# Strided q and k rows of batch 0: two a partition on 128 partitions and a short third transfer, in place of three a partition on 96

## The chip, the cores and the metric

The kernel runs on one core of a Trainium2 chip. The time is the device time of one execution in microseconds (us). Engines are called as the profile calls them: PE (TensorE matmul) and PEld (its weight loads), DVE (VectorE), ACT (ScalarE), POOL (GpSimd) and SP (SyncE). Transfers are issued by POOL or SP and carried by 16 DMA engines that all queues share.

## The reference

Eight batches of eight heads, 576 positions, 64 values a head, go through masked attention; the result, laid out as 4608 tokens of 512 values, goes through a two-layer network with a squared ReLU. Heads 0 to 3 look at the last 32 positions, heads 4 to 7 at earlier positions with the same remainder by 32 ("strided").

```python
scores = scale * np.matmul(q, k.transpose(0, 1, 3, 2))
rel = pos[:, None] - pos[None, :]
mask_local = (rel >= 0) & (rel < 32)
mask_strided = (rel >= 0) & (pos[None, :] % 32 == pos[:, None] % 32)
masks = np.stack([mask_local if h < H // 2 else mask_strided for h in range(H)], axis=0)
scores = np.where(masks[None, :, :, :], scores, -1000000000.0)
attn = softmax(scores)                       # over the last axis
x = np.matmul(attn, v).transpose(0, 2, 1, 3).reshape(B * S, H * D)
h = x @ w_in                                 # 512 -> 2048
out = np.maximum(h, 0.0) ** 2 @ w_out        # 2048 -> 512
```

## The kernel before

Work is cut into units (batch, pair of heads); units 0 and 1 of batch 0 are local, 2 and 3 strided. The network runs in nine chunks of 512 tokens: `mm1` (line 678, 64 matmuls a chunk) makes relu squared of `x @ w_in`, `mm2` (line 700) multiplies by `w_out`. Order is written by hand: each engine executes its instructions in program order. The string `BATCH0` lists the steps of the first batch, and `PLAN` lists which attention steps and which loads stand before which group of network matmuls.

Before `BATCH0` stands a setup. SP issues the q and k of unit 0 (`load_qk_hw`, line 275). POOL issues the strided q rows of batch 0 (`load_str_rows`, line 313), builds the identity matrix (`make_identity`), issues the strided k rows (line 313 again), and then cuts the two masks with three selects (lines 851 and 853 for `mask_loc`, 861 for `mask_str`). After these it issues q and k of unit 1 (line 295), v of batch 0 (lines 408 and 580) and the four quarters of `w_in` (line 429). DVE meanwhile fills constants and then turns the masks into additive biases in a corner of `w_out_b` (lines 863, 865, 866). Ten matmuls on zeros (`warm`, line 735) run on PE.

`BATCH0` then runs, on PE in this order: transposes of unit 0's q and k (line 457), after a cast by ACT for q and by DVE for k (line 302); scores of unit 0 (`S0`: bias matmul line 489, score matmuls line 500); the transposes of the strided rows, two groups for q (`W0q0`, `W0q1`) and two for k (`W0k0`, `W0k1`), by `step_TS` at line 336, with copies at line 341; scores of units 2, 3 and 1, sums and outputs; and `P0 P2 P13`, the first network matmuls. `w4`, `w2`, `w3` are more matmuls on zeros between them.

The strided rows: q (or k) of heads 4 to 7 of batch 0 is read as 288 rows of eight positions each, 512 values of fp32, cast to bf16 by the transfer, and lies in `w_out_b` at rows of blocks 4 to 6 (q) or 8 to 10 (k), where the later `w_out` has its place. Before, row 96*s + p is on partition p, block s. A transpose takes 128 columns of one block and all its partitions and puts them into 96 columns of a PSUM tile; six of them fill the 576 columns of a group.

Of the kernel before, what the change touches and what calls it, by code (L numbers as in the profile page):

```python
# [162 lines left out]
def kernel(  # L163
# [9 lines left out]
    nc = tc.nc  # L173
    B, H, S, D = q.shape
# [5 lines left out]
    QL = 96  # L180
    NL = S // QL
    NJ = 8
    RH = STRIDE // NJ
    SP_ = RH * NA
# [29 lines left out]
    def bank(nm):  # L214
        if places:
            return all_banks[places.pop(0)]
        t = banks[nm].pop(0)
        banks[nm].append(t)
        while id(t) in unread:
            run_due(lambda x: x[1] == unread[id(t)])  # L220
        return t
# [11 lines left out]
    ident = singles.tile([128, 128], BF16)  # L233
# [15 lines left out]
    w_out_b = singles.tile([128, 16, d_model], BF16)  # L249
# [52 lines left out]
        copy(t.rearrange("p j h d -> p h j d"), s[name + "f"].rearrange("p h (j d) -> p h j d", j=6))  # L302
        s[name] = t

    NP3 = 4 * SP_ // QL
    str_rows = {}

    def load_str_rows(b, name):
        src = q if name == "q" else k
        if b == 0:  # L310
            c = 4 if name == "q" else 8
            t = w_out_b[0:QL, c:c + NP3, :]
            nc.gpsimd.dma_start(out=t, in_=src[b, 4:8].rearrange("h (p j) d -> (h p) (j d)", j=NJ)
                                .rearrange("(s p) c -> p s c", p=QL))
        else:
            t = str_rows_t[name][0:SP_]
            nc.gpsimd.dma_start(out=t, in_=src[b, 4:8].rearrange("h (m r) d -> (h m) (r d)", r=STRIDE))
        str_rows[b, name] = t

    def step_TS(b, name, g, copy):  # L320
        src = str_rows[b, name]
        pt = bank("pt").bitcast(BF16)[:, 0:S]
        if b:
            for i in range(NJ):
                c = 128 * (NJ * g + i)
                nc.tensor.transpose(pt[:, SP_ * i:SP_ * (i + 1)], src[:, c:c + 128], ident[0:SP_, 0:SP_])
            if g == 0:
                o = strTs[name].tile([128, NP2 * SR], BF16, name=f"{name}T_s")
                str_T[b, name] = o.rearrange("c (a p) -> c a p", p=SR)
            copy(str_T[b, name][:, NJ * g:NJ * (g + 1), 0:SP_], pt.rearrange("c (a p) -> c a p", p=SP_))  # L330
            return
        for i in range(2):
            for s3 in range(NP3):
                c = 128 * (2 * g + i)
                o = S // 2 * i + QL * s3
                nc.tensor.transpose(pt[:, o:o + QL], src[:, s3, c:c + 128], ident[0:QL, 0:QL])
        if g == 0:
            o = strTs[name].tile([128, 2 * NJ * SR], BF16, name=f"{name}T_s")
            str_T[b, name] = o[:, 0:2 * NJ * SP_].rearrange("c (a r) -> c a r", a=NJ // 2)
        o = str_T[b, name]  # L340
        copy(o[:, 2 * g:2 * g + 2, :].rearrange("c a r -> c (a r)"), pt)
        if g == 1:
            for i in range(2):
                st.setdefault(2 + i, {})[name + "T"] = \
                    o[:, :, 2 * SP_ * i:2 * SP_ * (i + 1)].rearrange("c a (h p) -> c h a p", h=2)
# [397 lines left out]
    def run_step(word):  # L743
# [7 lines left out]
        elif op == "T":  # L751
            step_T(int(arg[:-2]), arg[-2], ENG[arg[-1]])
        elif op == "W":
            step_TS(int(arg[0]), arg[1], int(arg[2]), ENG[arg[3]])
        elif op == "S":
            u, _, half = arg.rstrip("!").partition(".")
# [19 lines left out]
        elif op == "P":  # L776
            first_part([int(x) for x in arg])
        elif op == "H":
            shift_v_local(int(arg[:-1]), ENG[arg[-1]])
        elif op == "C":  # L780
            load_str_tall(int(arg[:-1]), arg[-1])
        elif op == "Q":
            load_qk_rows(int(arg[:-1]), arg[-1])
        elif op == "X":
            transpose_str(int(arg[:-1]), arg[-1])
        elif op == "Y":
            transpose_local(int(arg))
        elif op == "V":
            load_v_local_all(int(arg))
        elif op == "U":  # L790
            load_v_str(int(arg))
        elif op == "B":
            spread_v_str(int(arg[0]), int(arg[1]), ENG[arg[2]])
        elif op == "l":
            load_qk_local_sw(int(arg[0]), [int(x) for x in arg[2:].split("+")], arg[1])
        elif op == "r":
            load_str_rows(int(arg[0]), arg[1])
        elif op == "i":
            load_w_in(int(arg))
        elif op == "o":  # L800
            load_w_out(int(arg))
        elif op == "z":
            late_constants()
        else:
            raise ValueError(word)
# [29 lines left out]
    nc.scalar.preload_act_table_set("natural_log_exp_and_others")  # L835
    load_qk_hw(0)
    load_str_rows(0, "q")
    make_identity(nc, ident)
    load_str_rows(0, "k")
    nc.vector.memset(idle, 0.0)  # L840
    nc.vector.memset(mask_loc, 1.0)
# [64 lines left out]
    for line in PLAN.strip().splitlines():  # L906
        n, words = line.split(":")
# [38 lines left out]
```

## Time and profile before

| | us |
|---|---|
| median of 3 runs (lowest to highest) | 303.32 (302.56 to 304.88) |
| the profiled execution's own time | 303.32 |
| its span in the profile | 301.6 |
| PE busy in the span | 294.5 (98%) |
| POOL busy in the span | 74.7 (25%) |
| first `mm1` matmul starts (from the span's start) | 18.44 |

The granted TensorE clock is 1.0 over the whole span. Times in the profile count from the span's start; the profiled execution has 1.72 us outside the span. In a timeline line the columns are: start, duration, engine, source line, operation, output<-inputs, shape, count; in brackets the idle time of the engine before it and what ended that. A matmul's duration includes a tail that overlaps the next one's, so the distance between starts tells the rate: four 128x512 matmuls in the chain take 0.86 us.

### The profile page before, as it was taken

To read this page: it belongs to the slowest core of one execution; us is meant where nothing else is said; L and a number is where in the kernel's file an instruction comes from. 1 tells how busy PE (TensorE), PEld (TensorE's weight loads), DVE (VectorE), ACT (ScalarE), POOL (GpSimd) and SP (SyncE) were. 2 spreads that over 40 slices of the span, in tenths; PEclk is the share of its full clock that TensorE was granted. 3 is DMA by queue.
4 is the path that set the end of the run, shared out by engine and by line. 5 is a ranking of instruction groups with operands and counts; after the bars stand their busy time and mean duration, and the time that the engine had idled before them with its cause. 6 is when DMAs were issued, how large, how long until landed. Compare 5 with 4: busy or idle time off the path is not lost.

```text
span 301.6 us, 5728 instructions
## 1 busy us (share of the span) xinstructions
PE 294.5 (98%) x2182; PEld 146.1 (48%) x2182; DVE 177.5 (59%) x456; ACT 174.2 (58%) x333; POOL 74.7 (25%) x107
## 2 busy tenths in 40 slices
PE   7999999999999999999999999999999999999996
PEld 3654554545545444444445445444454444444444
DVE  5576599588669676585568485666485524104400
ACT  3777846786658734874387447743875356226611
POOL 8755953007304026055301830000000000000000
PEclk9999999999999999999999999999999999999999
DMA  7999999998999999999999999511011110010011
GB/s 150 185 206 197 190 202 186 154 188 139 150 190 153 157 178 183 158 139 117 188 146 163 142 195 154 107 55 70 36 23 20 72 70 1 35 72 35 0 72 70
DMA packets 93643, 37.28 MB, mean 124 GB/s; under 512 B 78956, under 2 KB 87750, under 8 KB 93616
## 3 DMA queue, kind: packets, MB, share of 16 engines
q0 software_dynamic: 54960, 18.82, 63.6%
q1 hardware_dynamic: 38512, 18.03, 30.6%
q8 instruction: 17, 0.28, 0.4%
q14 instruction: 10, 0.08, 0.1%
q10 hardware_dynamic: 144, 0.07, 0.1%
HBM read 38.21 MB, written 9.44 MB: 158 GB/s over the span
## 4 chain that ended last, share of the span: by engine, by line
PE 73%; DMA 20%; POOL 3%; DVE 1%; issue 1%; ACT 0%; DVEq 0%; POOLq 0%; SPq 0%
PE psb L678 33%; PE psb L700 33%; DMA k_t<-in_k_dram 10%; DMA w_in_b<-in_moe_w_in_dram 4%; DMA xt<-x_l 3%; DMA kT_s<-k_t 3%; PE psb L638 1%; PE psb L725 1%; PE psb L546 1%; PE psb L500 1%; PE psb L560 1%; PE psb L557 1%; POOL xt L295 1%; POOL w_in_b L429 0%; POOL q_t L830 0%
## 5 line engine op out<-in xcount | busy, mean ns | idle before, releaser
L678 PE MATMUL psb<-xt,w_in_b 128*128 128x512 bf16 x576 | 132.9, 379 | 0.2 <-DMA xt<-x_l 0.2
L700 PE MATMUL psb<-w_out_b,g_sb 128*128 128x512 bf16 x560 | 128.8, 379 | 0.0
L684 ACT ACTIVATE r<-psb 128x512 bf16<-128x512 f32 x144 | 85.9, 598 | 34.9 <-PE psb L678 30.8
L685 DVE TENSOR_TENSOR g_sb<-r 128x512 bf16<-128x512 bf16 x144 | 60.3, 423 | 65.7 <-ACT r L684 64.7
L678 PEld LDWEIGHTS <-w_in_b 128*128 128x128 bf16 x576 | 53.0, 97 | 58.8 <-issue 1.0
L700 PEld LDWEIGHTS <-g_sb 128*128 128x128 bf16 x560 | 51.6, 98 | 56.9 <-DVE g_sb L685 0.5
L704 ACT COPY y<-psb 128x512 f32<-128x512 f32 x35 | 20.6, 589 | 53.7 <-PE psb L700 53.7
L570 DVE TENSOR_TENSOR xt<-psb,rv 64x144 bf16<-64x144 f32 x84 | 34.0, 405 | 17.5 <-ACT rv L563 16.4
L516 ACT ACTIVATE e<-psb 128x288 bf16<-128x288 f32 x56 | 20.0, 416 | 6.6 <-PE psb L500 6.6
L562 ACT ACTIVATE rv<-psb 128x432 f32<-128x432 f32 (+1 forms) x21 | 10.5, 502 | 11.1 <-PE psb L557 11.1
L644 DVE TENSOR_TENSOR x_l<-psb,rinv 96x384 bf16<-96x384 f32 x28 | 15.5, 554 | 1.0
L576 DVE TENSOR_TENSOR xt<-psb,rv 64x270 bf16<-64x270 f32 (+1 forms) x28 | 10.9, 432 | 8.5 <-ACT rv L563 8.3
L354 POOL DMA_DIRECT2D q_t<-in_q_dram x6 | 3.3, 556 | 44.8 <-DMA qT_s<-q_t 28.6
L522 DVE TENSOR_TENSOR e<-e,mask_all 128x576 bf16<-128x576 bf16 x28 | 12.3, 451 | 3.5 <-ACT e L516 3.2
L547 ACT ACTIVATE e<-psb 128x432 bf16<-128x432 f32 (+1 forms) x21 | 10.4, 497 | 5.7 <-PE psb L546 5.7
L423 POOL DMA_DIRECT2D vl<-in_v_dram x7 | 10.1, 1446 | 11.9 <-DMA vl<-in_v_dram 9.8
L283 POOL DMA_DIRECT2D q_l<-in_q_dram x16 | 11.6, 730 | 3.6 <-DMA k_t<-in_k_dram 1.9
L283 POOL DMA_DIRECT2D k_l<-in_k_dram x16 | 11.7, 738 | 1.8 <-DMA v_st<-in_v_dram 0.9
L563 ACT ACTIVATE rv<-rv 128x432 f32<-128x432 f32 (+1 forms) x21 | 11.2, 533 | 0.7
L638 PEld LDWEIGHTS <-e 128*128 128x128 bf16 x168 | 8.2, 97 | 5.8 <-DVE e L522 1.0
L638 PE MATMUL psb<-vl,e 128*128 128x65 bf16 x168 | 9.5, 193 | 0.8 <-DVE e L522 0.8
L354 POOL DMA_DIRECT2D k_t<-in_k_dram x6 | 3.2, 538 | 25.5 <-DMA kT_s<-k_t 25.5
(113 smaller groups left out, 210.7 us busy)
## 6 DMA issues: line engine op xcount, KB each, us to landing
out_dram<-y SPq DMA_DIRECT2D x35, 256.0 KB, 4.3
vl<-in_v_dram POOLq DMA_DIRECT2D x7, 384.0 KB, 13.3
w_in_b<-in_moe_w_in_dram POOLq DMA_DIRECT2D x4, 512.0 KB, 11.8
w_out_b<-in_moe_w_out_dram POOLq DMA_DIRECT2D x4, 512.0 KB, 14.2
q_t<-in_q_dram POOLq DMA_DIRECT2D x7, 288.0 KB, 5.7
k_t<-in_k_dram POOLq DMA_DIRECT2D x7, 288.0 KB, 7.2
v_st<-in_v_dram POOLq DMA_DIRECT2D x7, 216.0 KB, 8.1
k_l<-in_k_dram POOLq DMA_DIRECT2D x16, 72.0 KB, 7.7
```

What stands on the lines that cost most here:

```text
L283: nc.gpsimd.dma_start(out=t[:, :, hh, :], in_=src[b, 2 * p + hh].rearrange("(t p) d -> p t d", p=QL))
L516: nc.scalar.activation(e[0:kn, lo:lo + S // 2], pss[row][half][0:kn, 0:S // 2], AF.Exp, scale=scale)
L522: nc.vector.tensor_tensor(x, x, m, op=ALU.mult)
L563: nc.scalar.activation(rv, rv, AF.Exp, scale=-1.0)
L570: nc.vector.tensor_tensor(to[:, :, NJ * part:NJ * (part + 1), par], of, by, op=ALU.mult)
L638: nc.tensor.matmul(po[:, n, :], e[:, c:c + 128], rhs[:, NL * part + n, 0:D + 1], start=True, stop=True)
L644: nc.vector.tensor_tensor(x, po[0:QL, :, 0:D], rinv[0:QL].to_broadcast([QL, NL, D]), op=ALU.mult)
L678: nc.tensor.matmul(ph, w_in_b[:, kk, 128 * ff:128 * (ff + 1)], xt[kk][:, 512 * c:512 * (c + 1)], start=(kk == order[0]), stop=(kk == order ...
L684: nc.scalar.activation(r, ph, AF.Relu)
L685: later(1, lambda: nc.vector.tensor_tensor(g[:, ff, :], r, r, op=ALU.mult))
L700: nc.tensor.matmul(py, g[:, ff, 128 * j:128 * (j + 1)], w_out_b[:, ff, :], start=(ff == 0), stop=(ff == 15))
L704: nc.scalar.copy(y, py)
```

## The change

Each of the two loads of strided rows (q and k, batch 0) becomes two transfers. Rows 0 to 255 go to 128 partitions, row 128*s + p to partition p, block s (s = 0, 1); rows 256 to 287 go to partitions 0 to 31 of block 2. The transposes follow: for each 128 columns there are three, of 128, 128 and 32 rows, in place of three of 96. Bytes, rows and the number of transposes stay as they were; POOL issues two more transfers.

```diff
-    NP3 = 4 * SP_ // QL
+    NP3 = 3
...
         if b == 0:
             c = 4 if name == "q" else 8
-            t = w_out_b[0:QL, c:c + NP3, :]
-            nc.gpsimd.dma_start(out=t, in_=src[b, 4:8].rearrange("h (p j) d -> (h p) (j d)", j=NJ)
-                                .rearrange("(s p) c -> p s c", p=QL))
+            t = w_out_b[:, c:c + NP3, :]
+            rows = src[b, 4:8].rearrange("h (p j) d -> (h p) (j d)", j=NJ)
+            nc.gpsimd.dma_start(out=t[:, 0:2, :], in_=rows[0:256].rearrange("(s p) c -> p s c", p=128))
+            nc.gpsimd.dma_start(out=t[0:32, 2, :], in_=rows[256:288])
...
         for i in range(2):
-            for s3 in range(NP3):
+            for s3, n in enumerate((128, 128, 32)):
                 c = 128 * (2 * g + i)
-                o = S // 2 * i + QL * s3
-                nc.tensor.transpose(pt[:, o:o + QL], src[:, s3, c:c + 128], ident[0:QL, 0:QL])
+                o = S // 2 * i + 128 * s3
+                nc.tensor.transpose(pt[:, o:o + n], src[0:n, s3, c:c + 128], ident[0:n, 0:n])
```

## The prediction

> **What bounds the kernel now.** I read the busy table first: PE is busy 98% of the span. The waits of PE come next: after the first microseconds they are few and short, so from the first network matmul on the end is set by PE, and whatever starts that matmul later ends the kernel later, unless a wait further on swallows it. So I read the timeline of the first 19 us for what sets that start. These are its lines on the path; the weight load's is there for its wait.
>
> ```profile
> 1.36 0.83 POOL L313 DMA_DIRECT2D w_out_b<-in_q_dram  x1 [0.84 <-POOLq L930]
> 2.74 0.73 POOL L313 DMA_DIRECT2D w_out_b<-in_k_dram  x1
> 3.48 0.28 POOL L851 TENSOR_SCALAR_AFFINE_SELECT mask_loc<-mask_loc 128x96 bf16<-128x96 bf16 x1
> 4.13 0.33 DVE L863 TENSOR_SCALAR w_out_b<-mask_loc 128x576 bf16<-128x576 bf16 x1 [0.67 <-POOL mask_loc L853]
> 4.61 0.35 DVE L866 TENSOR_SCALAR w_out_b<-mask_str 72x288 bf16<-72x288 bf16 x1
> 5.10 0.56 DVE L302 CAST k_l<-g_sb 96x768 bf16<-96x768 f32 x1
> 5.71 0.43 PE L457 MATMUL psb<-ident,k_l 96*128 96x96 bf16 x6
> 6.99 0.30 PE L500 MATMUL psb<-qT,kTl 64*128 64x96 bf16 x6 [0.39 <-DVE kTl L464]
> 7.81 0.68 PE L336 MATMUL psb<-ident,w_out_b 96*128 96x96 bf16 x12
> 9.07 0.65 PEld L336 LDWEIGHTS <-w_out_b 96*128 96x128 bf16 x12 [0.21 <-DMA w_out_b<-in_k_dram]
> 17.09 0.65 POOL L398 DMA_DIRECT2D v_st<-in_v_dram  x1 [1.98 <-DMA w_in_b<-in_moe_w_in_dram]
> 18.44 10.53 PE L678 MATMUL psb<-xt,w_in_b 128*128 128x512 bf16 x48
> ```
>
> The path: POOL issues the two loads and the identity back to back, then cuts the masks. DVE sits 0.67 us until `mask_loc` is there, makes the biases, and only then, in program order, casts unit 0's k (5.10). Behind that cast stand its transposes, the copy, `S0`, and on PE all the rest of the first batch. From 10.85 on ACT is nearly without gaps up to 18.2, so nothing in between gives time back. The first network matmul starts at 18.44.
>
> The transfers are the second thing to read. The strided rows land 6.0 and 6.3 us after their issues, at 7.36 and 9.04; the first quarter of `w_in` lands by 17.09, where an issue on POOL is released by it. `w_in` was issued at 7.70, and the DMA share is 0.87 or more in every half microsecond from 2.5 on, so by then the transfers stand in a queue some microseconds long.
>
> ```profile
> w_out_b<-in_q_dram POOLq DMA_DIRECT2D x1, 288.0 KB, 6.0
> w_out_b<-in_k_dram POOLq DMA_DIRECT2D x1, 288.0 KB, 6.3
> L395 POOL DMA_DIRECT2D v_st<-in_v_dram x7 | 3.7, 531 | 4.5 <-DVE vb L402 3.1 <-DMA g_sb<-in_v_dram 1.3
> ```
>
> **Issues on POOL.** One load of 288 rows costs POOL 0.83 (q) or 0.73 us (k). The new pair is one of 256 rows and one of 32. For the larger, rows of 54 (0.53, the last line above) and 288 (0.73) are its neighbours; I take 0.03 less than now. For the 32 rows nothing in the trace is as small: it costs between 0 and 0.83, nearest to the 54 rows' 0.53, which I take. Extra: 0.50 us a name, 1.0 for both. Ends: 0 if an issue costs only by its rows (256 and 32 then make the old 288), 1.66 if the small one costs as much as the dearest old one and the large one saves nothing.
>
> What is queued behind them on POOL: the identity (ready 2.79, now 3.3; wanted at 5.0 by the transposes of q, so hidden), the three selects, and every later issue. The selects are not hidden: 4.10 becomes 5.1, line 863 starts 1.0 late, line 866 ends at 5.96. The cast of k before stood 0.14 us behind line 866 because its own load landed only then (1.27 plus 3.8 is 5.07); after, it starts right behind 866, at about 6.0: **0.9 late**, ends 0 and 1.6.
>
> **The later issues** move 1.0 with POOL (unit 1's q and k to 5.25 and 5.9, `w_in` to 8.7). That is covered by the queue: before, `w_in` waited from 7.70 to some 14 for its turn. On POOL an issue waits for the transfer eight before it (the thirteenth, `q_t` at 12.61, for the fifth, v; the fourteenth at 14.57 for the sixth; the fifteenth at 17.09 for the seventh). With two more in front the four of `w_in` wait for the four pieces of rows, landed by about 7.4 and 9.1 while their turn comes at 8.7 to 11; from the thirteenth old issue on the same pairs face each other. From 12.6 on POOL is in step with landings again and the 1.0 is gone there. Were that cover absent, `w_in` would land up to 1.0 later, 18.1 against a start that is itself late: still in time.
>
> **Transposes.** Twelve of 96 columns take 0.68, of which 0.206 is one alone: (0.68 - 0.206)/11 = 43 ns apart. Columns are 288 a set in both versions. By the column a 128 is 57 and a 32 is 14 ns; the twelve of 65 columns at line 620 come (0.54 - 0.193)/11 = 32 ns apart, so I price the 32-column one at 32. A set: 57 + 57 + 32 = 146 against 129, four sets a name, two names: 8 x 17 ns = **0.14** (ends 0 and 0.23, if the short one still takes 43). All of it is on PE's order. The rows themselves are not waited for: PE comes to the q transposes at 8.7 and to the k ones at about 10.1, one microsecond after today's landing. So the 0.21 of the weight load goes, and nothing is late after it.
>
> So the first network matmul starts 0.9 + 0.1 = 1.0 late, at 19.4.
>
> **What swallows part of it.** Later there is one place where PE waits, through DVE, for a transfer that this shift does not move.
>
> ```profile
> 64.18 0.38 DVE L370 COPY kb<-kT_s 64x864 bf16<-64x864 bf16 x1 [1.32 <-DMA kT_s<-k_t]
> 66.51 0.33 PE L638 MATMUL psb<-vl,e 128*128 128x65 bf16 x5
> 67.20 0.20 PE L638 MATMUL psb<-vl,e 128*128 128x65 bf16 x1 [0.36 <-DVE e L522]
> ```
>
> DVE sits 1.32 us until batch 2's transposed k lands (64.09). That load was issued at 39.68 by a POOL that had been busy without a gap since 30.7, so it stays. With the rest 1.0 late DVE reaches 64.18 with 0.3 to spare, and what follows there on DVE has its inputs in time. The sixth matmul could have followed the five after 5 x 32 ns, at 66.67; it started at 67.20: 0.53 us that a late PE does not lose. Behind it PE has no such hole but the 0.2 at 88.8, and that transfer hangs on PE's own results, so it moves along.
>
> Sum: 1.0 - 0.5 = **+0.5 us**. Against the profiled execution, 303.32 (span 301.6 and 1.72 around it), which is also the median shown: 303.8.
>
> **The pages weighed.** The row: transfers on POOL's queue land 0.7 us apart when they are 144 KB (unit 1's q and k, 4.25 and 4.92 plus 5.5 each), so no fixed time stands between two of them. The Trainium skill, "DMA: Bandwidth & Descriptors", Rules for kernel authors, says against this change that two transfers to disjoint partitions share the same engines and serialize, and in its Anatomy section fits about 2.0 us plus the bytes to each. By the row the two short transfers cost only their issue; by the page's fixed part, if it stood in line, k would be complete some 4 us later, at 13, and the sum would be near +3. The trace disagrees with that reading.
>
> **Rivals.**
> *The short transfers land late.* The smallest transfers here, 64 KB at the end, land 1.6 us after issue on an empty queue. Were both short ones to add that in line, k is complete at 9.04 + 3.2 = 12.2, PE waits 2.1 more at `W0k0`: 1.0 + 2.1 - 0.5 = +2.6, 305.9. It decides once k is complete after 10.1. Against it: the 0.7 above. 6%.
> *PE falls back to its slow rate.* The first warm matmuls start 0.427 apart, from about 4.3 us on 0.216. After the change PE idles from 5.5 to 6.5, longer than ever in this trace; if that costs the rate, the dense work needs 3 us again: the 48 matmuls lose 1.5, the steps from 8 to 18 some 1.5 more, in all +3.5, 306.8. Against it: after the 0.53 idle at 15 the warm matmuls at 16.97 are still 0.22 apart. 6%. By the Trainium skill, "TensorE: Matmul & The Clock Gate", The HAM clock gate, only an idle window of about 3.4 us drops the rate; by that it would not happen.
> *Not slower: the wider rows move faster, and the issue is cheap.* Between 5.5 and 6.5 the rows move at 122 GB/s, `w_in` on 128 partitions later at 200 and more. If it is the partitions, 590 KB take 2.9 in place of 4.8 us, every later landing comes 1.9 earlier, and the holes at 67 and 88.8 close by themselves (-0.7); if the issues also cost by their rows alone, nothing is lost in front: 302.6. It decides where the late start is under 0.5. Against it: unit 1's rows, on 96 partitions too, pass 147 KB in 0.7, 210 GB/s. 15%, with all that ends between -0.7 and +0.1.
> *The hole at 67 moves too* (transfers in step with POOL after all, as the page's chain of waits has it, which runs over the issues of `w_in`): nothing is swallowed, +1.0, 304.3. 20%.
>
> The forecast itself, +0.2 to +0.8, has 45%; the last 8% are sizes beyond these. The range of 8 in 10, from 302.6 to 305.4, takes in the last two rivals, the issue's upper end (1.66, so 1.6 + 0.2 - 0.5 = +1.3) and the spread of the runs shown (302.56 to 304.88). A difference of 1%, 3.0 us, is about what this kernel's measurement can tell from no change. Only the slow rate, and mishaps I have no row for, pass it upward: 0.09; downward hardly anything: 0.03; within: 0.88.
>
> **What would show it.** POOL: four issues at line 313, the short ones near 0.5; `mask_loc` ready at 5.1; cast of k near 6.0; k transposes near 10.1 with no wait for the rows; first `mm1` near 19.4; the 1.32 of DVE before 64.18 down to 0.3 and the 0.36 of PE gone. Wrong if the short issues cost far less, if a row piece lands after 10, or if the landings of `w_in` move.

## The result and the profile after

The changed kernel takes 304.80 us (median of 18 runs, 304.24 to 305.96) against 303.24 (18 runs, 302.56 to 306.2): a ratio of 1.0044, 95% interval 1.0023 to 1.0064. By the medians it is slower by 1.56 us, on the side that was forecast and inside the range (302.6 to 305.4), but three times the +0.5 that was worked out. Its profiled execution took 305.0 us with a span of 303.3, 1.7 more than before.

The timeline of the first 21 us, changed kernel (lines after 314 stand one lower in the code than before; the view ends at 30 us, so the count of the last line stops there):

```profile
1.27 4.45 PE L736 MATMUL psb<-xt 128*128 128x512 bf16 x10 [1.27 <-DVE xt L841]
2.21 0.53 POOL L315 DMA_DIRECT2D w_out_b<-in_q_dram  x1
4.01 0.52 POOL L315 DMA_DIRECT2D w_out_b<-in_k_dram  x1
5.18 0.33 DVE L864 TENSOR_SCALAR w_out_b<-mask_loc 128x576 bf16<-128x576 bf16 x1 [1.17 <-POOL mask_loc L854]
5.92 0.49 DVE L302 CAST k_l<-g_sb 96x768 bf16<-96x768 f32 x1
7.86 0.30 PE L501 MATMUL psb<-qT,kTl 64*128 64x96 bf16 x6 [0.39 <-DVE kTl L465]
8.68 1.41 PE L337 MATMUL psb<-ident,w_out_b 128*128 128x128 bf16 x12
10.89 1.40 PE L337 MATMUL psb<-ident,w_out_b 128*128 128x128 bf16 x12
20.95 9.25 PE L679 MATMUL psb<-xt,w_in_b 128*128 128x512 bf16 x41
```

The short issues cost POOL 0.53 and 0.52, the masks come 1.05 later, the cast at 5.92 (5.10 before), the scores at 7.86 (6.99). So far the forecast in its numbers. Then each set of twelve transposes lasts 1.41 and 1.40 us where it lasted 0.68, and the first network matmul starts at 20.95, 2.5 us after the 18.44 of before, not 1.0. The rows themselves are there when PE comes: the transfer issues of the changed kernel (KB, us to landing) put the last k rows at 4.01 + 5.1 = 9.1.

```profile
w_out_b<-in_q_dram POOLq DMA_DIRECT2D x1, 256.0 KB, 6.1
w_out_b<-in_k_dram POOLq DMA_DIRECT2D x1, 256.0 KB, 5.6
w_out_b<-in_q_dram POOLq DMA_DIRECT2D x1, 32.0 KB, 5.4
w_out_b<-in_k_dram POOLq DMA_DIRECT2D x1, 32.0 KB, 5.1
```

What the transposes do is seen in narrow windows of the timeline (a line begins with the first instruction that the window touches):

```profile
8.67 0.11 PEld L337 LDWEIGHTS <-w_out_b 128*128 128x128 bf16 x2
8.68 0.28 PE L337 MATMUL psb<-ident,w_out_b 128*128 128x128 bf16 x2
8.74 0.34 PE L337 MATMUL psb<-ident,w_out_b 128*128 128x128 bf16 x2
8.89 0.09 PEld L337 LDWEIGHTS <-w_out_b 32*128 32x128 bf16 x1
8.89 0.35 PE L337 MATMUL psb<-ident,w_out_b 32*128 32x32 bf16 x2
9.01 0.28 PE L337 MATMUL psb<-ident,w_out_b 128*128 128x128 bf16 x2
9.23 0.35 PE L337 MATMUL psb<-ident,w_out_b 32*128 32x32 bf16 x2
```

The second 128-row transpose starts 0.06 after the first, as priced. The 32-row one starts 0.15 after that, and the next 128-row one 0.12 later, although it follows only 32 columns. The weight loads show where the time goes: the two of 128 rows go back to back (8.67 to 8.78), the one of 32 rows begins only at 8.89, with its own matmul. A set of three takes 0.33 us, not 0.146.

Later, at the hole near 67, DVE and PE of the changed kernel show what the forecast wanted: DVE's wait is shorter and the 0.36 of PE is gone.

```profile
65.04 0.38 DVE L371 COPY kb<-kT_s 64x864 bf16<-64x864 bf16 x1 [0.58 <-DMA kT_s<-k_t]
68.77 0.36 PE L639 MATMUL psb<-vl,e 128*128 128x65 bf16 x6
```

To follow a late start through the kernel I take ACT's 181 evictions of network results, which every trace has in the same order, and subtract their start before from their start after. This is worked out from the traces; evictions are counted from 0: "first" is number 0 (20.37 before), "28" the one at 62.85, "34" at 70.22, "40" at 89.65, "end" the last.

| profiled execution | first | 28 | 34 | 40 | end |
|---|---|---|---|---|---|
| changed kernel | 2.52 | 2.26 | 1.72 | 1.71 | 1.71 |

So 0.26 is given back between 33 and 52 us, 0.54 near 67, and 1.7 arrives.

### The profile page after: what moved, and what is told of

The parts are those of the page before. It is cut to its first block, busy times and chain, and to the rows that moved or that the text cites. A ratio compares the mean times of both kernels' runs of the same rounds, so it can differ in the third digit from the quotient of the medians.

```text
span 303.3 us, 5692 instructions
## 1 busy us (share of the span) xinstructions
PE 294.4 (97%) x2144; PEld 147.4 (49%) x2182; DVE 177.1 (58%) x456; ACT 174.1 (57%) x333; POOL 75.7 (25%) x109
## 4 chain that ended last, share of the span: by engine, by line
PE 90%; DVE 3%; DMA 3%; issue 1%; ACT 1%; DVEq 0%
PE psb L679 41%; PE psb L701 35%; DMA xt<-x_l 3%; PE psb L736 2%; PE psb L501 2%; PE psb L639 2%; PE psb L547 1%; PE psb L726 1%; PE psb L458 1%; PE psb L561 1%; PE psb L558 1%; DVE xt L571 1%; PE psb L337 1%; PE psb L490 1%; DVE kb L371 0%
## 5 line engine op out<-in xcount | busy, mean ns | idle before, releaser
L701 PE MATMUL psb<-w_out_b,g_sb 128*128 128x512 bf16 x542 | 126.2, 379 | 1.3 <-issue 0.5
```

The source lines that it names most:

```text
L701: nc.tensor.matmul(py, g[:, ff, 128 * j:128 * (j + 1)], w_out_b[:, ff, :], start=(ff == 0), stop=(ff == 15))
```

## The experiments

Expectations were written with the theory that POOL's issues cost 0.87 through the masks, the changes of height in the transposes 1.65, and the holes give back 0.8. The rivals: PE runs at its slow rate in that stretch, transposes of 128 rows are slow by themselves, or the issues are the whole loss. The kernel before was run beside each; all ratios are to it, with 95% intervals.

**The two issues alone.**

```diff
-            nc.gpsimd.dma_start(out=t, in_=src[b, 4:8].rearrange("h (p j) d -> (h p) (j d)", j=NJ)
-                                .rearrange("(s p) c -> p s c", p=QL))
+            rows = src[b, 4:8].rearrange("h (p j) d -> (h p) (j d)", j=NJ)
+            nc.gpsimd.dma_start(out=t[:, 0:2, :], in_=rows[0:192].rearrange("(s p) c -> p s c", p=QL))
+            nc.gpsimd.dma_start(out=t[:, 2, :], in_=rows[192:288])
```

> Layout and transposes of before (three rows a partition on 96), but each load issued as two transfers (192 rows, 96 rows). My theory now: of the changed kernel's late first network matmul (21.1 against 18.4) 0.87 us come from POOL's two extra issues, by the masks, DVE's biases and its cast of k; the rest from the transposes. Then here: first score matmuls of unit 0 near 7.9 (6.99 before), twelve transposes still 0.52 us from the first to the next instruction, first network matmul near 19.3. Of this 0.87 the holes behind it swallow most: total +0 to +0.4 us, ratio 1.000 to 1.0015. Rival (the extra issue accounts for the whole loss, the transposes lose nothing at the end): +1.5, ratio 1.005.

Measured: 303.29 against 303.03, ratio 1.0028 (1.0003 to 1.0053). Timeline of this kernel:

```profile
5.86 0.49 DVE L302 CAST k_l<-g_sb 96x768 bf16<-96x768 f32 x1
8.77 0.69 PE L337 MATMUL psb<-ident,w_out_b 96*128 96x96 bf16 x12
19.40 10.54 PE L679 MATMUL psb<-xt,w_in_b 128*128 128x512 bf16 x48
```

Casts, scores and transposes are where the theory put them, the first matmul is 0.96 late, and of that 0.14 is left at the end of the trace. The ratio is above the expected 1.000 to 1.0015, though the medians differ by 0.26 us only: it goes with the means (303.97 against 303.09), and four of the twelve executions took 304.5 to 306.5. By the medians the issues alone cost less than the whole change (0.26 against 1.56 us); by the ratios, whose intervals overlap, that is not shown.

**Fewer changes of height.** The 128-row transposes of a group first: 8 changes in all in place of 16.

```diff
-        for i in range(2):
-            for s3, n in enumerate((128, 128, 32)):
+        for i, s3, n in ((0, 0, 128), (0, 1, 128), (1, 0, 128), (1, 1, 128), (0, 2, 32), (1, 2, 32)):
```

> The changed kernel, but in each group of twelve columns blocks' transposes the 128-row ones come first and the 32-row ones last, so the number of rows changes 8 times in all in place of 16. My theory: a change of the number of rows between two neighbouring transposes costs about 0.1 us (128 to 32: 0.155 between starts, 32 to 128: 0.115, 128 to 128: 0.06). Then a pair of groups takes 0.93 in place of 1.34 us, the first network matmul starts near 20.2, total 0.8 under the changed kernel: ratio to before 1.001 to 1.003. Rival 1 (PE is at its slow rate there): the order does not matter, 1.34 and 21.1 stay, ratio 1.0044. Rival 2 (transposes of 128 rows are slow by themselves): the same, 1.34 stays.

Measured: 304.3 against 303.03, ratio 1.0043 (1.0028 to 1.0059). Timeline:

```profile
8.56 1.01 PE L336 MATMUL psb<-ident,w_out_b 128*128 128x128 bf16 x12
10.38 1.00 PE L336 MATMUL psb<-ident,w_out_b 128*128 128x128 bf16 x12
20.05 10.12 PE L678 MATMUL psb<-xt,w_in_b 128*128 128x512 bf16 x46
```

The same 24 transposes, in another order, take 1.0 a set in place of 1.4. A slow rate or slow 128-row transposes would not depend on the order: both rivals fall. The first matmul stands at 20.05, 20.2 expected. The total missed: 0.8 less than the changed kernel was expected, and by the medians (1.27 against 1.56 over before) it is 0.3 less; the intervals of the two ratios overlap, so not even this 0.3 is shown. Its profiled execution ended 1.05 after before.

**The short issues behind the masks.**

```diff
-            nc.gpsimd.dma_start(out=t[0:32, 2, :], in_=rows[256:288])
+            short.append((t[0:32, 2, :], rows[256:288]))
...
                             base=0, channel_multiplier=-1, pattern=[[1, SP_]])
+    for t, rows in short:
+        nc.gpsimd.dma_start(out=t, in_=rows)
```

> The changed kernel, with both 32-row transfers issued behind the three mask selects on POOL. My theory: the masks are ready at 4.1 again, DVE casts unit 0's k at 5.1, the scores start near 7.0; the short k rows land before PE wants them (by 9.5). The transposes keep their 1.34 us a pair. First network matmul near 20.2, total 0.85 under the changed kernel, ratio to before 1.001 to 1.003. Rival (a short transfer issued later lands late): PE waits for rows at its k transposes, and the first network matmul stays near 21.

Measured: 304.79, ratio 1.0052 (1.0035 to 1.0068). The rival was right in the total, but PE waits at the q transposes, not at those of k. Timeline:

```profile
4.79 0.56 DVE L302 CAST k_l<-g_sb 96x768 bf16<-96x768 f32 x1
7.29 0.30 PE L502 MATMUL psb<-qT,kTl 64*128 64x96 bf16 x6 [0.39 <-DVE kTl L466]
9.41 1.19 PE L338 MATMUL psb<-ident,w_out_b 32*128 32x32 bf16 x10 [1.01 <-DMA w_out_b<-in_q_dram]
21.47 8.81 PE L680 MATMUL psb<-xt,w_in_b 128*128 128x512 bf16 x40
```

The scores start at 7.29 in place of 7.86, but the short q rows, issued at 4.28, stand in the queue behind the 256 k rows (landed at 9.2) and land at 9.4; PE waits 1.01 for 32 rows. Here the short issue cost 0.5 us where it stood first, and more when it was moved back.

**Both, and all heights sorted** (4 changes in all): the short issues as above, and the groups of a name together.

```diff
+        todo = [(g, i, s3, 128) for i in range(2) for s3 in range(2)]
+        if g == 1:
+            todo += [(gg, i, 2, 32) for gg in range(2) for i in range(2)]
+        for gg, i, s3, n in todo:
...
+        for gg in range(2):
+            pts[gg][1](o[:, 2 * gg:2 * gg + 2, :].rearrange("c a r -> c (a r)"), pts[gg][0])
```

> Both together, and all eight 128-row transposes of a name before its four 32-row ones: the number of rows changes 4 times in all. My theory: a name takes 0.7 us (0.52 before, 1.34 in the changed kernel), the first network matmul starts between 18.8 and 19.0, and the 0.4 to 0.6 that it is late are swallowed later: total +0 to +0.2 us, ratio 0.999 to 1.001. Rivals 1 and 2 (slow rate, slow 128-row transposes): a name keeps 1.34, first network matmul near 20.2, ratio 1.001 to 1.003.

Measured: 304.0, ratio 1.0037 (1.0016 to 1.0058). That is above the expected 0.999 to 1.001. The k set lasts 0.80, by the height theory once more, and the first matmul stands at 19.37, later than the 19.0 expected; 0.08 of it is a wait for the short q rows (the first of them starts 0.23 after the transpose before it, against 0.15 elsewhere). The end of the trace is 0.98 late, not level:

```profile
9.90 0.80 PE L344 MATMUL psb<-ident,w_out_b 128*128 128x128 bf16 x12
65.52 0.38 DVE L380 COPY kb<-kT_s 64x864 bf16<-64x864 bf16 x1 [1.50 <-DMA kT_s<-k_t]
68.54 0.20 PE L648 MATMUL psb<-vl,e 128*128 128x65 bf16 x1 [0.38 <-DVE e L532]
```

Here batch 2's transposed k let DVE go on only at 65.52, 1.34 later than before, and the hole that should have given time back took some.

**How much of a late start is given back.** The kernel before, with more matmuls on zeros ahead of the last steps of the first batch (`w3/5` becomes `w7/5`, then `w15/5`).

> The kernel before with four more matmuls on zeros just before the last steps of the first batch: the first network matmul starts 0.86 later (19.3), nothing else of the first batch changes. It measures how much of a late start is given back. My theory: the holes where PE waits for transfers that do not move (near 67 above all) swallow 0.5 to 0.9: total +0 to +0.4 us. Rival (nothing is swallowed): +0.86, ratio 1.0028.

> The same with twelve more matmuls on zeros: 2.6 later (21.0), as late as in the changed kernel. My theory: the holes swallow up to 0.9 and the rest comes through: total +1.7 us, ratio 1.0056, the changed kernel's own. Rival (nothing is swallowed): +2.6, ratio 1.0086.

Measured: 303.44 against 303.06, ratio 1.0003 (0.9985 to 1.0021), and 305.12, ratio 1.0063 (1.0041 to 1.0086). By the ratios, of 0.79 late (first matmul at 19.23) nearly nothing arrives, of 2.79 (21.23) about 1.9: 0.7 to 0.9 are free, as expected, and the second dose costs about what the change does. Lags for four more: 0.79 first, 1.03, 0.50, 0.12, 0.13. In the profiled execution of the second dose (309.78 us) PE fell back to half rate for 6.8 us, as the last section shows, so its lags are left out.

**One move only: the k pair behind the masks, and the same with the heights sorted.**

```diff
     make_identity(nc, ident)
-    load_str_rows(0, "k")
...
                             base=0, channel_multiplier=-1, pattern=[[1, SP_]])
+    load_str_rows(0, "k")
```

> The changed kernel with one move: both k transfers of the strided rows are issued behind the three mask selects, so that the q pair alone stands ahead of the masks. All transposes as in the changed kernel. My theory (issues cost through the masks, transposes cost by the changes of height): masks ready near 4.1, scores of unit 0 start at 7.0, the q rows are there in time (issued as in the changed kernel, landed by 7.7), k rows land by 9.9, just before PE wants them at 10.0; the transposes keep 1.34 us a name, so the first network matmul is 1.65 late, at 20.1. Of that 0.8 is given back: total +0.8 to +1.2, ratio 1.0025 to 1.004. Rival (the transposes' time is swallowed as a whole, the loss is the issues'): ratio under 1.001.

Measured: 304.8 against 303.27, ratio 1.0042 (1.0018 to 1.0067). The masks were early, and the scores late all the same:

```profile
1.27 4.45 PE L736 MATMUL psb<-xt 128*128 128x512 bf16 x10 [1.27 <-DVE xt L840]
5.07 0.56 DVE L302 CAST k_l<-g_sb 96x768 bf16<-96x768 f32 x1 [0.49 <-DMA g_sb<-in_k_dram]
7.96 0.30 PE L501 MATMUL psb<-qT,kTl 64*128 64x96 bf16 x6 [0.24 <-DVE kTl L465]
```

The cast is at 5.07 as before, but the ten warm matmuls take 4.45 us where the trace of before has 3.92: PE is still at half rate, and its early transposes and warm matmuls hold up the scores. The trace's record of PE's clock steps to full at 7.29 here, at 6.73 in the changed kernel's trace and at 4.52 in that of before. So the 0.87 that I had read off the two traces and put on the masks could be the clock's.

> The same move, and the eight 128-row transposes of each name ahead of its four 32-row ones. Both costs are small now: transposes 0.73 a name (0.52 before), so the first network matmul starts near 18.9, 0.45 late, about as the prediction priced the transposes alone. Total: that is given back at 67 and 88, ratio 0.999 to 1.001. Rival (something else of the change, the transfers' own order or landing, costs 1 us later in the kernel, as the last trace of both mends together hints, where batch 2's transposed k landed 1.3 later than before): ratio 1.003 with a first network matmul that is only 0.5 late.

Measured: 304.47, ratio 1.0035 (1.0015 to 1.0055), although the profiled execution, with its first network matmul at 19.16, ended 0.09 ahead of before. The ratio is the rival's, not the theory's.

**Further executions of two kernels, nothing edited.**

> The kernel before, another profiled execution. Theory: where PE's full rate comes later than the 4.5 us of the profile shown, the scores of unit 0 start up to 1 us later (8.0 at most), the first network matmul as much, and the end moves by 0.2 at most, because that lag is given back at 65 to 70 and at 88. Rival: the end moves as far as the first network matmul.

> As the second look at before: a third execution, for how far the step of PE's rate and batch 2's transposed k move by themselves. Theory: the step lies anywhere between 4.2 and 7.6, the landing of the transposed k between 63.5 and 65.5, and the end within 0.3 of the first trace. Rival: the end moves by as much as the first network matmul does.

> The kernel of e6 once more, for another profiled execution: its first one ended level with before, its median 1.2 us later. Theory now: PE's step from its slow to its full rate comes at a different moment in each execution (between 4.2 and 7.3 us in the traces so far) and moves the scores of unit 0 by up to 1 us; before has 0.8 us of late start free, this kernel has used 0.5 to 0.7 of them. Then here the end's lag is the first network matmul's lag less about 0.85, and nothing below zero. Rival: the lag at the end comes from batch 2's transposed k (landing later than 64.2), whatever the first network matmul does.

> As the second look. A third execution of the same kernel: the theory wants the lags at the end ordered as the lags of the first network matmul; the rival wants them ordered as the landing of batch 2's transposed k.

Single times: before 306.36 and 303.05, the other 304.55 and 303.89. Timeline of the second look at before:

```profile
1.27 4.45 PE L735 MATMUL psb<-xt 128*128 128x512 bf16 x10 [1.27 <-DVE xt L840]
5.31 0.63 DVE L302 CAST k_l<-g_sb 96x768 bf16<-96x768 f32 x1 [0.35 <-DMA g_sb<-in_k_dram]
7.86 0.30 PE L500 MATMUL psb<-qT,kTl 64*128 64x96 bf16 x6 [0.39 <-DVE kTl L464]
66.79 0.38 DVE L370 COPY kb<-kT_s 64x864 bf16<-64x864 bf16 x1 [1.42 <-DMA kT_s<-k_t]
```

With the step at 6.77 the unchanged kernel starts its scores at 7.86, to the hundredth where the changed one did with its step at 6.73. And here the transposed k came at 66.79. All traces but that of the second dose side by side (step: when the record of PE's clock goes to full; scores: first matmul of line 500, a line or some further down in the edited kernels; kb: start of DVE's first copy of batch 2's transposed k; lags as above):

| kernel | step | scores | kb | first | 28 | 34 | end |
|---|---|---|---|---|---|---|---|
| before | 4.52 | 6.99 | 64.18 | 0 | 0 | 0 | 0 |
| before, second | 6.77 | 7.86 | 66.79 | 0.87 | 1.00 | 2.61 | 3.07 |
| before, third | 6.20 | 7.58 | 62.98 | 0.59 | 0.66 | 0.12 | -0.24 |
| four more on zeros | 4.19 | 6.99 | 64.65 | 0.79 | 1.03 | 0.50 | 0.13 |
| two issues alone | none recorded | 7.95 | 64.50 | 0.97 | 1.03 | 0.50 | 0.14 |
| changed kernel | 6.73 | 7.86 | 65.04 | 2.52 | 2.26 | 1.72 | 1.71 |
| heights sorted by group | 5.05 | 7.75 | 64.03 | 1.64 | 1.94 | 1.41 | 1.05 |
| short issues behind masks | 5.57 | 7.29 | 64.53 | 3.04 | 2.44 | 1.91 | 1.57 |
| both, sorted by name | 5.76 | 7.38 | 65.52 | 0.94 | 1.06 | 1.34 | 0.98 |
| k pair behind masks | 7.29 | 7.96 | 64.91 | 2.62 | 2.38 | 1.84 | 2.16 |
| the same, sorted by name | 4.94 | 7.08 | 63.36 | 0.72 | 0.79 | 0.26 | -0.09 |
| second look at it | 4.16 | 7.44 | 65.33 | 0.91 | 1.25 | 1.15 | 1.25 |
| third look at it | 6.47 | 7.72 | 63.95 | 1.30 | 1.48 | 0.94 | 0.59 |

One rule, found in these rows, fits every one of them: the lag at 34 is the larger of two numbers, the lag at 28 less 0.53 or 0.54, and kb less 64.18. For the second look at before it is 66.79 - 64.18 = 2.61; for the changed kernel 2.26 - 0.54 = 1.72. It also fits the trace of the second dose, which is not in the table: 7.40 at 28 less 0.53 is its 6.87 at 34. Both theories of the last expectations were half right: the three executions of the sorted kernel are ordered neither by the first matmul alone nor by the landing alone, but by whichever is later. Before's third look ended 0.24 off with a first matmul 0.59 late, as expected; its second one ended 3.07 off, which neither expectation had. In both the transposed k came outside the 63.5 to 65.5 expected (66.79 and 62.98).

## Why the prediction was right in sign and short in size

**PE sets the end, by its first network matmul:** right. In every trace the lag after 90 us stays to the end within 0.04 us (the changed kernel's 1.71 at 40 is 1.71 at the last).

**Issues on POOL, 0.50 a name:** right (0.53 and 0.52 for the short ones; masks 1.05 later). The later issues were covered only in that PE waited neither for rows nor for `w_in`. The forecast had POOL level again from 12.6 on, and named moved landings of `w_in` as a sign of being wrong. In the changed kernel the issue on POOL that waits for the first quarter of `w_in` comes at 18.77 in place of 17.09, and the one ahead of it at 16.25 in place of 14.57. In the second look at before these stand at 18.45 and 15.92, so how much of this the change does is open.

**The cast and all behind it 0.9 late:** the number came (0.87), but the step is only half of it. It took the scores' 6.99 as fixed. They are where the cast or PE's clock allows, whichever is later: with the cast at 5.07 to 5.31 they ranged from 6.99 to 7.96, mostly by the step of the clock. With late masks they start at 7.75 even with an early step (heights sorted, step 5.05, against 7.08 for masks on time and a step at 4.94): the masks then cost 0.67. With a step near 6.7 they cost nothing: 7.86 in the changed kernel and in the second look at before. That the profile of before showed one throw of this was not seen.

**Transposes, 0.14 (0 to 0.23):** this is the step that failed, and its upper end with it. The two sets cost 1.64: from the first transpose to what follows on PE, 1.34 and 1.33 against 0.52 and 0.51 (behind the q set the first matmul on zeros is missing from the trace; its place is taken from the spacing of the others). I priced columns only. What was left out is the change of height between neighbouring weights: 0.15 on the way from 128 to 32 rows and 0.12 back, in place of 0.06 from 128 to 128 and 0.025 from 32 to 32, so about 0.095 a change. 16 changes make 1.5, and with the 0.14 that was priced that is about the 1.64 measured. The sorted orders show it: 16 changes 1.4 a set, 8 changes 1.0, 4 changes 0.8.

In these experiments columns change together with rows. The trace of before separates them, and it could have been read beforehand:

```profile
60.05 2.75 PE L678 MATMUL psb<-xt,w_in_b 128*128 128x512 bf16 x12
62.74 0.43 PE L500 MATMUL psb<-qT,kTl 64*128 64x96 bf16 x12
63.10 1.04 PE L678 MATMUL psb<-xt,w_in_b 128*128 128x512 bf16 x4
63.98 0.42 PE L457 MATMUL psb<-ident,q_l 96*128 96x96 bf16 x6
64.23 1.98 PE L678 MATMUL psb<-xt,w_in_b 128*128 128x512 bf16 x8
```

Behind twelve matmuls from 60.05 on, 0.2155 apart, the next could start at 62.64; the first with weights of 64 rows starts 0.10 later, at 62.74. Behind four from 63.10 on the next could start at 63.96, and the first transpose with weights of 96 rows does, at 63.98. Both are 96 columns wide. In the whole trace of before the first score matmul of line 500 starts 0.311 or 0.312 us after a 512-column matmul at all 13 such places, and the way back takes 0.133 to 0.135; at line 457 it is 0.215 or 0.216 at eight of nine places (at the ninth PE waits), and back 0.042 or 0.043. So it is not every change of rows that costs: between 128 and 96 there is no cost here, between 128 and 64 or 32 some 0.09 to 0.10 us each way.

**The hole at 67, 0.53:** the size was right, and is the best-measured number here: 0.53 or 0.54 in all nine traces of the table that came late and found the transposed k in time. The reason given, that the load was issued at 39.68 by a busy POOL and so stays, was wrong. The load that DVE waits for is issued by SP, at 56.10 in the trace of before, as soon as the load of batch 2's k ahead of it has landed (56.02); that one is POOL's, at 39.68. In the changed kernel POOL issued it at 41.63, 1.95 later, and it landed at 55.99 all the same. In the other two executions of before it landed at 58.87 and 54.55, and DVE's copy moved with it, to 66.79 and 62.98. Beside the hole 0.24 to 0.60 was given back between 33 and 52 us by the three latest starts, and 0.36 to 0.38 at 88 in eight of the twelve traces compared with the first, though not in the changed kernel's. I had called that a hole that moves along.

The sum, with what was measured: 0.87 + 1.64 - 0.26 - 0.54 = 1.71, the span's difference of 1.7; the medians say 1.56. The forecast's +0.5 had 1.0 in front and 0.5 given back: the late start was 2.5, the hole as it was priced.

**The rivals.** Short transfers landing late: not in the changed kernel, but it is what the third experiment made happen. Slow rate: PE didn't fall back; it rose late, which no rival had. Faster wide rows: all q rows had landed by 7.6 and all k rows by 9.1, against 7.36 and 9.04 before, so they were no faster. The hole moving too: not in the changed kernel's trace, where 0.54 was given back there; but in three of the twelve (second look at before, both sorted by name, second look at the sorted one) the late transposed k decided.

**What stays open.** What makes the first network matmul late is shown: the changes of height, and the masks or the step of the clock, whichever holds up the scores. That this lateness is what costs 1.56 us fits the profiled execution, but is not shown for the medians. Four more matmuls on zeros made it 0.79 late and the median 0.38 longer; the versions with all heights sorted made it 0.93 and 0.72 late and the median 0.97 and 1.20 longer. With both costs nearly gone the change still shows 1.0037 and 1.0035, and halving the height changes moved the median by 0.3 where 0.8 was expected. The traces say that a late transposed k decides part of the executions, before's as well; whether the change of batch 0's loads makes that landing later on average, three executions of each can't tell. No version tried beat the kernel before.

## What to carry to other kernels

Count how often neighbouring matmuls go from tall weights to short ones and back (here 128 rows to 64 or 32; 128 to 96 was free), not only their columns: filling more partitions made taller transposes beside short ones, and the changes to the short remainder cost 1.5 us. A transfer that nothing waits for still pays for its issue where something on the path stands behind it on the same engine (0.5 us here), and issuing it later can cost more (1.0 here). Before you read a difference of some tenths off two traces, look at a second trace of the unchanged kernel.

## What the runs showed of the hardware

The moment at which PE goes to its full rate differs from one execution to the next of the same program: 4.52, 6.77 and 6.20 us for before, 4.16 to 7.29 over all, though the warm matmuls start at 1.27 in each. The Trainium skill, "TensorE: Matmul & The Clock Gate", Part 1: The HAM clock gate, says that the activity window is about 3.4 us long and free-running, so that the transition depends on where in it the first matmul lands; the spread of 3.1 us here agrees with it. The ±500 ns from run to run that the same section of the Trainium skill gives is too small for these executions. The clock column of a profile reads 1.00 ahead of the step too, because the record of these traces only begins with it; the step itself is seen in the matmuls on zeros, 0.43 apart ahead of it and 0.22 behind it.

It can fall again as well: in the profiled execution with twelve more matmuls on zeros PE waited from 33.7 to 35.7 us for a cast, and the clock fell to half in that wait, at 34.92. The prediction set against its slow-rate rival the rule of the Trainium skill that only an idle window of about 3.4 us drops the rate. This trace does not agree: the wait was 2.0 us long, and PE was busy for 45% of the 3.4 us ahead of the fall. It is one execution. The table by stretches of this kernel has as columns the stretch, its length, busy time and count of PE, PEld, DVE, ACT and POOL, then the granted clock, the DMA share and GB/s; the clock reads 1.00, 0.50, 1.00.

```profile
30.00:34.90 4.90, 3.05 (x19) 1.15 (x16) 4.46 (x7) 3.62 (x6) 4.81 (x5) 1.00 1.54 190
34.90:41.70 6.80, 5.80 (x45) 3.41 (x46) 2.60 (x5) 2.46 (x5) 1.23 (x2) 0.50 1.44 199
41.70:50.00 8.30, 7.94 (x98) 4.62 (x97) 6.69 (x17) 5.39 (x14) 2.93 (x4) 1.00 1.53 185
```

And from start to start PE needs 0.15 us from a 128-row transpose to a 32-row one and 0.12 for the way back, against 0.06 between 128-row transposes and 0.025 to 0.04 between 32-row ones. From 128 to 64 rows and back it is about 0.10 and 0.09 more than the columns take, from 128 to 96 and back nothing.
